# Attention's norms leave GpSimd for ACT and VectorE, its last stores go to GpSimd's queue, and the warming matmuls get fewer and longer

## The chip, the core and the metric

The kernel runs on one core of a Trainium2 chip. Time is device time in microseconds (us), from the profiler or from runs without it. A core has five engines with queues of their own: TensorE (PE in the profile; its weight loads are PEld), VectorE (DVE), ScalarE (ACT), GpSimd (POOL) and SyncE (SP, which here only issues transfers). SP, ACT and GpSimd each issue DMAs on queues of their own (SPq, ACTq, POOLq). Each engine works its instructions in order; semaphores join them.

## The reference, cut

```
q_n, k_n = rmsnorm(q, g_q), rmsnorm(k, g_k)      # 8 batches, 12 heads, 448 tokens, 64 wide
attn = softmax(q_n @ k_n.T / sqrt(64))
x = (attn @ v) as 3584 tokens x 768
logits = x @ w_gate                               # 8 experts
expert = argmax(logits); gate = softmax(logits)[expert]
for e in 8 experts:                               # the 80 tokens with the largest gate
    out[tok] = gate[tok] * (relu(x[tok] @ w1[e]) @ w2[e])
```

`rmsnorm(x, g)` is `x / sqrt(mean(x * x) + 1e-6) * g`. All other rows of `out` are zero.

## The kernel before

Attention works in 24 groups of four heads (three groups to a batch), `NG = 24`. A group has seven rounds of score and exponential (`RD = 7`), and two rounds make a slot, so a batch takes 10.5 slots and the loop 84. A table written out by hand (`begins`, `mid`, `end`, each a list of calls per slot) says what is issued in which slot; each engine's queue keeps that order. In a slot TensorE makes the scores of two rounds (`score`, L332), ACT takes their exponentials (L335), VectorE adds up the ones of the slot before (`presum`, L359 and L361), and TensorE multiplies these by v (`av`, L347). At a group's end ACT copies the product to `us` (L352), which the next group's product waits for, since it uses the same PSUM tile `po`.

A group's q and k (index `a` is 0 and 1) are normalised ahead of its first round `b0`: ACT squares (`square`, L254), VectorE sums over 64 columns (`rstd`, L263) and scales the mean (L265), GpSimd raises it to -1/2 (L272), and GpSimd multiplies q or k by it (`normalise`, L287; VectorE for group 1). TensorE transposes the product (`transp`, L299) and ACT copies it out. Group 0 goes in halves, with a square root on ACT (L269) and a reciprocal on VectorE, and its second halves are multiplied on GpSimd.

After a batch's last group the gate is computed: `zl` on TensorE, two copies on ACT, their sum `zsb` on VectorE (L389), transposes `zt` on TensorE, then on VectorE the products `lx` and the logits, whose exponential `lex` ACT takes (L445). A merge of the batch's tokens into the list of the best 80 per expert follows over six slots (`merge`): `beat`, `tied`, `ahead`, `rnk`, `rank`, `put` and `keep` on VectorE, counts and placing on TensorE (L584, L588). GpSimd computes the small table `info` for it (L463 to L480).

GpSimd's queue also carries the weights. `fetch_w1` and `fetch_w2` bring three experts' weights into SBUF as bf16 (L180, L184), `stage_w` writes the other five to a DRAM scratch (L190), from which SP's queue fetches them late (`fetch_late`, L196). SP's queue loads q, k and v and stores the attention's rows to `xr_scratch`. After the loop comes the last batch's ranking, with matmuls between that have no result (`busy`, L754), then gathers of the chosen rows by GpSimd (L860), and the eight experts (L894, L912).

Of the kernel before, what the change touches and what calls it, by code (L numbers as in the profile page):

```python
# [20 lines left out]
def kernel(  # L21
# [13 lines left out]
    nc = tc.nc  # L35

    B, H, S, D = q.shape
# [16 lines left out]
    NG = B * NQ  # L54
    NB = 2 * NX
# [11 lines left out]
    cpool = ctx.enter_context(tc.tile_pool(name="const", bufs=1))  # L67
# [49 lines left out]
    nc.vector.memset(eps[:, :], 1e-6)  # L117
    nhalf = cpool.tile([128, NB], F32, name="nhalf")
    nc.vector.memset(nhalf[:, :], -0.5)
    zsb = cpool.tile([128, 512], F32, name="zsb")  # L120
# [96 lines left out]
    with av_stack:  # L217
# [3 lines left out]
        st = [dict() for _ in range(NG)]  # L221
# [34 lines left out]

        def rstd(g, a, parts=ALLB):
            if "rs%d" % a not in st[g]:
                st[g]["ms%d" % a] = prep.tile([128, NB], F32, tag=f"ms{a}", name="ms")
                st[g]["rs%d" % a] = prep.tile([128, NB], F32, tag=f"rs{a}", name="rs")  # L260
            ms, rs = st[g]["ms%d" % a], st[g]["rs%d" % a]
            for lo, hi in parts:
                nc.vector.reduce_sum(out=ms[:, lo:hi], in_=st[g]["sq%d" % a][:, lo:hi], axis=AX.X)  # L263
                if parts is ALLB:
                    nc.vector.tensor_scalar(ms[:, lo:hi], ms[:, lo:hi], 1.0 / D, 1e-6,  # L265
                                            op0=ALU.mult, op1=ALU.add)
            for lo, hi in parts:
                if parts is not ALLB:
                    nc.scalar.activation(rs[:, lo:hi], ms[:, lo:hi], AF.Sqrt, scale=1.0 / D,  # L269
                                         bias=eps[:, :])  # L270
                else:
                    nc.gpsimd.tensor_tensor(rs[:, lo:hi], ms[:, lo:hi], nhalf[:, lo:hi],  # L272
                                            op=ALU.pow)

        def inverse(g, a, parts):
            for lo, hi in parts:
                rs = st[g]["rs%d" % a][:, lo:hi]
                nc.vector.reciprocal(rs, rs)  # L278

        def normalise(g, a, parts=ALLB):  # L280
            if "qn%d" % a not in st[g]:
                st[g]["qn%d" % a] = qkpool.tile([128, NB, D], F32, tag=f"qn{a}", name="qn", bufs=2)
            qn, qk, rs = st[g]["qn%d" % a], st[g]["qk"][a], st[g]["rs%d" % a]
            eng = nc.gpsimd if g > 1 or parts is HALF[1] else nc.vector
            for lo, hi in parts:
                h0, h1 = lo // NX, hi // NX
                eng.tensor_mul(  # L287
                    qn[:].rearrange("p (x hh) d -> p hh x d", hh=2)[:, h0:h1],
                    qk[:, lo:hi].rearrange("p (hh x) d -> p hh x d", x=NX),
                    rs[:, lo:hi].rearrange("p (hh x) -> p hh x", x=NX)  # L290
                    .unsqueeze(3).to_broadcast([128, h1 - h0, NX, D]))
# [110 lines left out]
        def gate1v(b):  # L402
# [80 lines left out]
        def merge(b):  # L483
# [29 lines left out]
            def vtied():  # L513
                gw, row = m["gw"], m["row"]
                nc.vector.tensor_tensor(tied[:], row[:, :].rearrange("p (j c) -> p j c", j=NT),
                                        gw.unsqueeze(2).to_broadcast([128, NT, 128]),
                                        op=ALU.is_equal)
                nc.vector.tensor_mul(tied[:], tied[:],
                                     tri[:, :].unsqueeze(1).to_broadcast([128, NT, 128]))

# [80 lines left out]
        def xout(g, u):  # L601
# [48 lines left out]
        for f, *a in ((square, 0, lo), (square, 0, hi), (rstd, 0, lo), (square, 1, lo),  # L650
                      (rstd, 0, hi), (square, 1, hi), (inverse, 0, lo), (normalise, 0, lo),
                      (inverse, 0, hi), (normalise, 0, hi), (rstd, 1, lo), (rstd, 1, hi),
                      (inverse, 1, lo), (normalise, 1, lo), (inverse, 1, hi),
                      (normalise, 1, hi), (transp, 0, 0), (transp, 0, 1), (gains, ),
                      (exptable, ), (transp, 1, 0)):
            at_slot(mid, -10, f, *([0] if a else []), *a)
        for g in range(NG):
# [101 lines left out]
    m, NT = gst[b], NJ + 1  # L759
    busy(35)  # L760
    gate2(b)
# [22 lines left out]
    busy(20)  # L784
    ahead = tpool.tile([128, NT, CAP], BF16, tag="ahead", name="ahead")
    for j in range(NT):
# [10 lines left out]
    nc.vector.tensor_tensor(tied[:], row[:, :].rearrange("p (j c) -> p j c", j=NT),  # L797
                            gw.unsqueeze(2).to_broadcast([128, NT, 128]), op=ALU.is_equal)
    nc.vector.tensor_mul(tied[:], tied[:], tri[:, :].unsqueeze(1).to_broadcast([128, NT, 128]))
    R, back = psb[:, 1, :NT * E], psa[:CAP, 0, :E]  # L800
    for i in range(NT):
# [3 lines left out]
        if i == 0:  # L805
            for j in range(NT):
# [3 lines left out]
    nc.vector.tensor_scalar(stay[:, :], back, rowF[:CAP, NT:NT + 1], float(CAP),  # L810
                            op0=ALU.add, op1=ALU.is_lt)
    left = tpool.tile([CAP, 5, E], BF16, name="left")
    nc.vector.tensor_mul(left[:], stay[:, :].unsqueeze(1).to_broadcast([CAP, 5, E]), listn[:])
# [31 lines left out]
    nc.vector.tensor_add(gwT[:, :], gwT[:, :], num[:, 2])  # L845
    busy(60)
    ps_stack.close()
# [112 lines left out]
```

## Time and profile before

| | us |
|---|---|
| median of 3 runs | 499.72 |
| lowest and highest | 498.36, 500.84 |
| the profiled execution's own time | 497.44 |
| its span, first to last instruction | 495.4 |
| TensorE's granted clock, mean | 0.968 of full speed |

The profile is that of one execution. Its own time is the span and some 2 us around it, and the sums below are made against it.

### The profile page before, as it was taken

Reading aid. Unit: us, or ns where it says so; the run is one execution under the profiler, and the core shown is the slowest. Engines: PE = TensorE matmul, PEld = TensorE weight load, DVE = VectorE, ACT = ScalarE, POOL = GpSimd, SP = SyncE. Lnnn points to the kernel's source line nnn. Section 1 sums busy time; section 2 is a strip of 40 time slices with the busy share of each in tenths; the row PEclk is TensorE's granted clock in tenths of the full one; section 3 lists DMA queues with packets and bytes.
Section 4 is the critical chain, followed back from the end, with each engine's and each line's share of the span. In section 5 each row is a group of like instructions: output and inputs, shape, how many; then the busy total and the mean of one; then the engine's idle time right before and its main releaser. Section 6 shows DMA issues by size and latency. Waiting matters only on the chain. (4 is left out here: it accounts for less than half of the span.)

```text
span 495.4 us, 11552 instructions
## 1 busy us (share of the span) xinstructions
PE 446.8 (90%) x4721; PEld 224.5 (45%) x4721; DVE 368.7 (74%) x569; ACT 317.1 (64%) x489; POOL 269.6 (54%) x210
## 2 busy tenths in 40 slices
PE   6979999999899999898899999898999998659991
PEld 6334434443344444443344444343444443457880
DVE  5769748996889789967799689867897876623540
ACT  6857877966677779676787788666877774101120
POOL 3686983848366748835757678376377400151111
PEclk9989999999899999989999999998999999978996
DMA  7389979697759895977399979958767795957922
GB/s 242 112 179 271 243 180 251 151 295 163 225 80 242 200 271 121 275 199 150 111 232 214 274 167 234 281 109 207 168 167 175 175 268 182 366 139 271 423 69 60
DMA packets 68283, 100.84 MB, mean 204 GB/s; under 512 B 8328, under 2 KB 60040, under 8 KB 66952
## 3 DMA queue, kind: packets, MB, share of 16 engines
q1 hardware_dynamic: 51184, 70.05, 43.4%
q0 software_dynamic: 15776, 29.13, 33.5%
q10 hardware_dynamic: 1272, 0.94, 0.6%
q8 instruction: 37, 0.61, 0.5%
q14 instruction: 14, 0.11, 0.1%
HBM read 101.11 MB, written 39.89 MB: 285 GB/s over the span
## 5 line engine op out<-in xcount | busy, mean ns | idle before, releaser
L272 POOL TENSOR_TENSOR rs<-ms,nhalf 128x14 f32<-128x14 f32 x46 | 136.2, 2964 | 128.6 <-DVE ms L265 125.0
L335 ACT ACTIVATE at<-ps 128x896 f32<-128x896 f32 x168 | 146.4, 922 | 17.7 <-PE ps L332 17.7
L361 DVE TENSOR_TENSOR sm<-sm,at 128x896 f32<-128x896 f32 x120 | 153.1, 1276 | 6.1 <-DVE sm L361 0.5
L332 PE MATMUL ps<-qkT 64*64 64x448 f32 x1344 | 150.1, 557 | 2.3 <-ACT zo L387 1.5
L347 PE MATMUL po<-at,vt 64*64 64x448 f32 x1344 | 146.1, 544 | 6.3 <-ACT us L352 6.3
L347 PEld LDWEIGHTS po<-at,vt 64*64 64x64 f32 x1344 | 49.8, 134 | 79.4 <-issue 66.6
L287 POOL TENSOR_TENSOR qn<-qk,rs 128x896 f32<-128x896 f32 (+1 forms) x46 | 80.8, 1770 | 4.8 <-DVE rs L278 4.4
L263 DVE TENSOR_REDUCE ms<-sq 128x14 f32<-128x896 f32 (+1 forms) x50 | 52.0, 1043 | 29.8 <-ACT sq L254 26.9
L332 PEld LDWEIGHTS ps<-qkT 64*64 64x64 f32 x1344 | 43.4, 134 | 67.9 <-issue 39.7
L299 PE MATMUL tp<-ident,qn 128*128 128x128 f32 x336 | 53.8, 285 | 5.3 <-POOL qn L287 4.0
L299 PEld LDWEIGHTS tp<-ident,qn 128*128 128x128 f32 x336 | 38.5, 144 | 19.6 <-issue 7.1
L254 ACT ACTIVATE sq<-qk 128x896 f32<-128x896 f32 (+1 forms) x50 | 45.9, 923 | 1.4 <-DMA qk<-in_q_dram 1.4
L613 ACT COPY xb<-xp 128x512 f32<-128x512 f32 x48 | 28.3, 590 | 17.9 <-PE xp L608 12.2
L389 DVE TENSOR_TENSOR zsb<-zsb,zo 128x448 f32<-128x448 f32 x7 | 21.3, 3039 | 23.4 <-ACT zo L387 23.4
L898 ACT ACTIVATE h_sb<-ph 128x320 bf16<-128x320 f32 x16 | 6.9, 437 | 47.0 <-PE ph L894 45.9
L320 ACT ACTIVATE qkT<-tp,gqk 128x512 f32<-128x512 f32 (+1 forms) x46 | 29.5, 643 | 6.9 <-PE tp L299 6.9
L608 PE MATMUL xp<-ident,us 128*128 128x128 f32 x192 | 31.8, 290 | 0.0
L608 PEld LDWEIGHTS xp<-ident,us 128*128 128x128 f32 x192 | 21.2, 144 | 21.5 <-issue 17.1
L322 ACT COPY qkT<-tp 128x512 f32<-128x512 f32 (+1 forms) x46 | 24.8, 539 | 7.1 <-PE tp L299 6.9
L920 POOL DMA_INDIRECT out_dram<-yo,idxT x8 | 7.6, 953 | 36.4 <-DVE yo L915 13.5
L352 ACT COPY us<-po 128x896 f32<-128x896 f32 x24 | 21.7, 904 | 7.0 <-PE po L347 7.0
L359 DVE TENSOR_TENSOR sm<-at 128x896 f32<-128x896 f32 x24 | 26.0, 1084 | 0.1
(170 smaller groups left out, 440.8 us busy)
## 6 DMA issues: line engine op xcount, KB each, us to landing
wb_scratch<-in_moe_w_dram POOLq DMA_DIRECT2D x20, 768.0 KB, 8.6
w_sb<-wb_scratch SPq DMA_DIRECT2D x10, 1536.0 KB, 10.8
vt<-in_v_dram SPq DMA_DIRECT2D x24, 448.0 KB, 6.3
out_dram<-zeros SPq DMA_DIRECT2D x28, 384.0 KB, 9.0
qk<-in_q_dram SPq DMA_DIRECT2D x23, 448.0 KB, 7.1
qk<-in_k_dram SPq DMA_DIRECT2D x23, 448.0 KB, 7.7
w_sb<-in_moe_w_dram POOLq DMA_DIRECT2D x6, 1536.0 KB, 16.1
xr_scratch<-xb SPq DMA_DIRECT2D x46, 192.0 KB, 4.1
```

Source lines behind the costliest of these rows:

```text
L254: nc.scalar.activation(st[g]["sq%d" % a][:, lo:hi], st[g]["qk"][a][:, lo:hi], AF.Square)
L263: nc.vector.reduce_sum(out=ms[:, lo:hi], in_=st[g]["sq%d" % a][:, lo:hi], axis=AX.X)
L272: nc.gpsimd.tensor_tensor(rs[:, lo:hi], ms[:, lo:hi], nhalf[:, lo:hi], op=ALU.pow)
L287: eng.tensor_mul(qn[:].rearrange("p (x hh) d -> p hh x d", hh=2)[:, h0:h1], qk[:, lo:hi].rearrange("p (hh x) d -> p hh x d", x=NX), rs[:, ...
L299: nc.tensor.transpose(tp[:, x * 128:(x + 1) * 128], qn[:, 2 * (x0 + x):2 * (x0 + x) + 2].rearrange("p h d -> p (h d)"), ident[:, :])
L320: nc.scalar.activation(o, i, AF.Copy, scale=gqk[:, :])
L332: nc.tensor.matmul(ps[u * 64:u * 64 + 64, hh, :S], T1[d, u, x * 64:(x + 1) * 64], T0[d, u, :], start=True, stop=True)
L335: nc.scalar.activation(at[:], ps[:, :, :S], AF.Exp)
L347: nc.tensor.matmul(po[hh * D:(hh + 1) * D, u, :S], vt[p, hh * NX + x, :], at[p, hh, :], start=(x == 0), stop=(x == RD - 1))
L361: nc.vector.tensor_add(s["sm"][:], s["sm"][:], s["at%d" % x][:])
L608: nc.tensor.transpose(xp[:, j * 128:(j + 1) * 128], us[:, u, c:c + 128], ident[:, :])
L613: nc.scalar.copy(xb[:, :, u * 128:(u + 1) * 128], xp[:, :].rearrange("p (j d) -> p j d", d=128))
```

## The change

The power on GpSimd goes. `rstd` now takes q's and k's means together (28 columns): ACT takes the logarithm and an exponential of minus half of it, and VectorE makes one Newton step of three instructions. The reduction has a function of its own (`squares`), as has group 0's root (`root`). `normalise` is always VectorE's. In the slots, the reductions stay, `rstd` stands in the middle of slot `b0-5`, and group 1's normalisations move back by a slot. The table of functions that ACT loads before the loop has both the logarithm and the exponential. The last group's stores (`xr_scratch` from `rz` and `xb`) move from ACT's queue to GpSimd's. `tied` is made in four instructions of one operation each, not in two over all columns, and at the end it comes after `stay`. The matmuls of `busy` take 512 columns instead of 128, and 9, 5 and 22 of them stand for 35, 20 and 60.

```diff
+        def squares(g, a, parts=ALLB):
...
+                nc.vector.reduce_sum(out=st[g]["ms"][:, a, lo:hi],
+                                     in_=st[g]["sq%d" % a][:, lo:hi], axis=AX.X)
...
-                    nc.gpsimd.tensor_tensor(rs[:, lo:hi], ms[:, lo:hi], nhalf[:, lo:hi],
-                                            op=ALU.pow)
+        def rstd(g):
+            ms, rs, nw = (st[g][n][:].rearrange("p a n -> p (a n)") for n in ("ms", "rs", "nw"))
+            nc.scalar.activation(rs, ms, AF.Ln, scale=1.0 / D, bias=eps[:, :])
+            nc.scalar.activation(rs, rs, AF.Exp, scale=-0.5)
+            nc.vector.scalar_tensor_tensor(nw, rs, -0.5 / D, rs, op0=ALU.mult, op1=ALU.mult)
+            nc.vector.scalar_tensor_tensor(nw, ms, D * 1e-6, nw, op0=ALU.add, op1=ALU.mult)
+            nc.vector.scalar_tensor_tensor(rs, nw, 1.5, rs, op0=ALU.add, op1=ALU.mult)
...
-            eng = nc.gpsimd if g > 1 or parts is HALF[1] else nc.vector
...
-                eng.tensor_mul(
+                nc.vector.tensor_mul(
...
-                (nc.sync if b < B - 1 else nc.scalar).dma_start(
+                (nc.sync if b < B - 1 else nc.gpsimd).dma_start(
...
-            eng = nc.sync if g < NG - 1 else nc.scalar
+            eng = nc.sync if g < NG - 1 else nc.gpsimd
...
+            nc.scalar.preload_act_table_set("natural_log_exp_and_others")
...
+                late = 3 if g == 1 else 0
                 for a in range(2):
-                    late = 3 if g == 1 else 0
                     at_slot(mid, b0 - 7 + a + late, square, g, a)
-                    at_slot(end, b0 - 7 + a + late, rstd, g, a)
-                    at_slot(mid, b0 - 5 + a + min(late, 2), normalise, g, a)
+                    at_slot(end, b0 - 7 + a + late, squares, g, a)
+                at_slot(mid, b0 - 5 + late, rstd, g)
+                for a in range(2):
+                    at_slot(mid, b0 - 5 + a + late, normalise, g, a)
...
-            nc.tensor.matmul(hot[:, :128], identb[:, :], identb[:, :], start=True, stop=True)
+            nc.tensor.matmul(hot[:, :], identb[:, :],
+                             tri[:, :].unsqueeze(1).to_broadcast([128, 4, 128]),
+                             start=True, stop=True)
...
+    for j in range(NT):
+        nc.vector.scalar_tensor_tensor(
+            tied[:, j], row[:, j * 128:(j + 1) * 128], gw[:, j:j + 1], tri[:, :],
+            op0=ALU.is_equal, op1=ALU.mult)
```

What the change does to the order on the engines shows at three places. The first is GpSimd's queue at the start of the program, behind its constants. Before:

```order
L169 MEMSET beat 128x4x64
L164 AFFINE_SELECT tri<-tri 128x128
L287 TENSOR_TENSOR qn<-qk,rs 128x7x64 x2
L272 TENSOR_TENSOR rs<-ms,nhalf 128x14 x4
L180 DMA w_sb<-in_moe_w_dram 128x6x1024
L287 TENSOR_TENSOR qn<-qk,rs 128x2x7x64 x2
L272 TENSOR_TENSOR rs<-ms,nhalf 128x14 x2
```

And with the change:

```order
L167 MEMSET beat 128x4x64
L162 AFFINE_SELECT tri<-tri 128x128
L178 DMA w_sb<-in_moe_w_dram 128x6x1024
L182 DMA w_sb<-in_moe_w_dram 128x8x768
L178 DMA w_sb<-in_moe_w_dram 128x6x1024
L464 TENSOR_SCALAR pt<-numF 128x4
```

Three weight fetches now stand right behind the constants, with nothing ahead of them; the next stand behind the first batch's gate (`pt`).

The second place is VectorE between the second batch's `zsb` and its `lex`. Before:

```order
L389 TENSOR_TENSOR zsb<-zsb,zo 128x448
L361 TENSOR_TENSOR sm<-sm,at 128x896 x4
L409 RECIPROCAL rz<-zs 128x12x2 x2
L417 TENSOR_TENSOR lx<-zs,rz 128x12x8 x4
L263 TENSOR_REDUCE ms<-sq 128x14
L265 TENSOR_SCALAR ms<-ms 128x14
L432 TENSOR_REDUCE lg<-lx 128x32
L435 TENSOR_REDUCE lmax<-lg 128x4
L438 TENSOR_TENSOR lex<-lg,lmax 128x32
```

And with the change (`nw` is the Newton step's own tile):

```order
L390 TENSOR_TENSOR zsb<-zsb,zo 128x448
L362 TENSOR_TENSOR sm<-sm,at 128x896 x2
L273 SCALAR_TENSOR_TENSOR nw<-rs 128x28
L274 SCALAR_TENSOR_TENSOR nw<-ms,nw 128x28
L275 SCALAR_TENSOR_TENSOR rs<-nw,rs 128x28
L288 TENSOR_TENSOR qn<-qk,rs 128x2x7x64
L362 TENSOR_TENSOR sm<-sm,at 128x896 x2
L288 TENSOR_TENSOR qn<-qk,rs 128x2x7x64
L410 RECIPROCAL rz<-zs 128x12x2 x2
L418 TENSOR_TENSOR lx<-zs,rz 128x12x8 x4
```

Two normalisations and a Newton step have moved in between; the reduction, `lg` and `lex` follow as before.

The third place is ACT behind the last group, where `us` is the last product's copy. Before:

```order
L352 COPY us<-po 128x896
L383 COPY zsb<-zl 128x448
L613 COPY xb<-xp 128x4x128
L424 DMA xr_scratch<-rz 64x4x12
L424 DMA xr_scratch<-rz 64x3x12
L613 COPY xb<-xp 128x4x128
L621 DMA xr_scratch<-xb 64x3x256 x2
L622 DMA xr_scratch<-xb 64x256
L445 ACTIVATE lex<-lex 128x32
L770 COPY eqT<-pse 24x512
```

And with the change:

```order
L353 COPY us<-po 128x896
L384 COPY zsb<-zl 128x448
L613 COPY xb<-xp 128x4x128 x2
L446 ACTIVATE lex<-lex 128x32
L776 COPY eqT<-pse 24x512
```

The five stores are gone from ACT's order; in GpSimd's they stand ahead of the last batch's `pt` and `info`.

## Rows read from the trace of the kernel before

**Rows 1.** The page's first part: busy us (share of the span), instructions.
```profile
PE 446.8 (90%) x4721; PEld 224.5 (45%) x4721; DVE 368.7 (74%) x569; ACT 317.1 (64%) x489; POOL 269.6 (54%) x210
```

**Rows 2.** Groups by shape: line, engine, operation, count | busy us, mean ns.
```profile
L361 DVE TENSOR_TENSOR sm<-sm,at 128x896 f32<-128x896 f32 x120 | 153.1, 1276 | 6.1 <-DVE sm L361 0.5
L359 DVE TENSOR_TENSOR sm<-at 128x896 f32<-128x896 f32 x24 | 26.0, 1084 | 0.1
L389 DVE TENSOR_TENSOR zsb<-zsb,zo 128x448 f32<-128x448 f32 x7 | 21.3, 3039 | 23.4 <-ACT zo L387 23.4
L569 DVE SCALAR_TENSOR_TENSOR rank<-rank,cnt 128x4 f32<-128x4 f32 x7 | 5.6, 799 | 0.2
L837 DVE SCALAR_TENSOR_TENSOR idxF<-num 80x8 f32<-80x8 f32 x1 | 0.2, 164 | 0.0
L287 DVE TENSOR_TENSOR qn<-qk,rs 128x896 f32<-128x896 f32 x2 | 2.2, 1092 | 3.3 <-POOL rs L272 3.3
L269 ACT ACTIVATE rs<-ms,eps 128x7 f32<-128x7 f32 x4 | 1.2, 297 | 0.9 <-DVE ms L263 0.9
L272 POOL TENSOR_TENSOR rs<-ms,nhalf 128x14 f32<-128x14 f32 x46 | 136.2, 2964 | 128.6 <-DVE ms L265 125.0 <-PE ps L332 3.0
```

**Rows 3.** Waits: engine, line, released by: us in total, times, longest.
```profile
PE po L347 <- ACT us L352: 6.3, 3, 2.1
PE tp L299 <- POOL qn L287: 4.0, 3, 3.0
PE mp L584 <- DVE put L572: 3.8, 3, 1.8
PE zt L394 <- DVE zsb L389: 3.7, 4, 1.2
PE mp L588 <- DVE keep L576: 1.2, 3, 0.4
```

**Rows 4.** In order of time, an odd batch's gate: start us, us, engine, line.
```profile
119.51 4.14 DVE L389 TENSOR_TENSOR zsb<-zsb,zo 128x448 f32<-128x448 f32 x1 [2.77 <-ACT zo L387]
131.61 0.23 ACT L445 ACTIVATE lex<-lex 128x32 f32<-128x32 f32 x1 [2.70 <-DVE lex L438]
```

**Rows 5.** In order of time, the start: ACT, TensorE, SP's DMA queue.
```profile
14.69 1.79 ACT L254 ACTIVATE sq<-qk 128x896 f32<-128x896 f32 x2
16.83 1.73 ACT L335 ACTIVATE at<-ps 128x896 f32<-128x896 f32 x2
17.33 0.98 PE L299 MATMUL tp<-ident,qn 128*128 128x128 f32 x7
29.97 0.81 PE L299 MATMUL tp<-ident,qn 128*128 128x128 f32 x4 [3.04 <-POOL qn L287]
7.86 0.37 SPq L226 DMA_DIRECT2D qk<-in_q_dram  x1
```

**Rows 6.** First weight fetch; loads issued in 16:19 and 70:75, us to landing.
```profile
27.10 1.09 POOL L180 DMA_DIRECT2D w_sb<-in_moe_w_dram  x1
qk<-in_q_dram SPq DMA_DIRECT2D x1, 448.0 KB, 3.6
qk<-in_q_dram SPq DMA_DIRECT2D x1, 448.0 KB, 12.7
```

**Rows 7.** The end in order of time, and its stores' landing (420:434).
```profile
424.33 1.25 ACTq L621 DMA_DIRECT2D xr_scratch<-xb  x2
426.32 0.23 ACT L445 ACTIVATE lex<-lex 128x32 f32<-128x32 f32 x1 [2.02 <-issue]
434.44 0.17 DVE L840 TENSOR_SCALAR idxG<-idxF 80x8 uint32<-80x8 f32 x1
xr_scratch<-xb ACTq DMA_DIRECT2D x2, 192.0 KB, 9.0
```

**Rows 8.** Matmuls of the first and second expert, in order of time.
```profile
444.69 3.36 PE L894 MATMUL ph<-xgT,w_sb 128*128 128x80 bf16 x48 [4.05 <-issue]
451.80 1.88 PE L894 MATMUL ph<-xgT,w_sb 128*128 128x80 bf16 x48
```

More of the change, by code (lines that the diff above doesn't have):

```diff
@@ L117 @@
     nc.vector.memset(eps[:, :], 1e-6)
-    nhalf = cpool.tile([128, NB], F32, name="nhalf")
-    nc.vector.memset(nhalf[:, :], -0.5)
     zsb = cpool.tile([128, 512], F32, name="zsb")
@@ L255, in square, with root @@
                                      AF.Square)
[L257 to L261, printed above, removed]
+        def squares(g, a, parts=ALLB):
+            if "ms" not in st[g]:
+                for n in ("ms", "rs", "nw"):
+                    st[g][n] = prep.tile([128, 2, NB], F32, tag=n, name=n)
             for lo, hi in parts:
[L263 to L266, printed above, removed]
+                nc.vector.reduce_sum(out=st[g]["ms"][:, a, lo:hi],
+                                     in_=st[g]["sq%d" % a][:, lo:hi], axis=AX.X)
+        def root(g, a, parts):
             for lo, hi in parts:
[L268 to L271, printed above, removed]
-                    nc.gpsimd.tensor_tensor(rs[:, lo:hi], ms[:, lo:hi], nhalf[:, lo:hi],
-                                            op=ALU.pow)
+                nc.scalar.activation(st[g]["rs"][:, a, lo:hi], st[g]["ms"][:, a, lo:hi], AF.Sqrt,
+                                     scale=1.0 / D, bias=eps[:, :])
+        def rstd(g):
[5 more added lines that the diff above has]
+            nc.vector.scalar_tensor_tensor(rs, nw, 1.5, rs, op0=ALU.add, op1=ALU.mult)
         def inverse(g, a, parts):
             for lo, hi in parts:
-                rs = st[g]["rs%d" % a][:, lo:hi]
+                rs = st[g]["rs"][:, a, lo:hi]
                 nc.vector.reciprocal(rs, rs)
@@ L282, in normalise @@
                 st[g]["qn%d" % a] = qkpool.tile([128, NB, D], F32, tag=f"qn{a}", name="qn", bufs=2)
-            qn, qk, rs = st[g]["qn%d" % a], st[g]["qk"][a], st[g]["rs%d" % a]
-            eng = nc.gpsimd if g > 1 or parts is HALF[1] else nc.vector
+            qn, qk, rs = st[g]["qn%d" % a], st[g]["qk"][a], st[g]["rs"][:, a]
             for lo, hi in parts:
                 h0, h1 = lo // NX, hi // NX
-                eng.tensor_mul(
+                nc.vector.tensor_mul(
                     qn[:].rearrange("p (x hh) d -> p hh x d", hh=2)[:, h0:h1],
@@ L514, in vtied @@
                 gw, row = m["gw"], m["row"]
[L515 to L519, printed above, removed]
+                for j in range(NT):
+                    nc.vector.scalar_tensor_tensor(
+                        tied[:, j], row[:, j * 128:(j + 1) * 128], gw[:, j:j + 1], tri[:, :],
+                        op0=ALU.is_equal, op1=ALU.mult)
             def experts():
@@ L645, in exptable @@
         def exptable():
+            nc.scalar.preload_act_table_set("natural_log_exp_and_others")
             nc.scalar.activation(warm[:, 0:1], warm[:, 1:2], AF.Exp)
         lo, hi = HALF
[L650 to L653, printed above, removed]
+        for f, *a in ((square, 0, lo), (square, 0, hi), (squares, 0, lo), (root, 0, lo),
+                      (square, 1, lo), (squares, 0, hi), (root, 0, hi), (square, 1, hi),
+                      (inverse, 0, lo), (normalise, 0, lo), (inverse, 0, hi),
+                      (normalise, 0, hi), (squares, 1, lo), (root, 1, lo), (squares, 1, hi),
+                      (root, 1, hi), (inverse, 1, lo), (normalise, 1, lo), (inverse, 1, hi),
                       (normalise, 1, hi), (transp, 0, 0), (transp, 0, 1), (gains, ),
@@ L753, in busy @@
         for i in range(n):
-            nc.tensor.matmul(hot[:, :128], identb[:, :], identb[:, :], start=True, stop=True)
+            nc.tensor.matmul(hot[:, :], identb[:, :],
+                             tri[:, :].unsqueeze(1).to_broadcast([128, 4, 128]),
+                             start=True, stop=True)
     b = B - 1
     m, NT = gst[b], NJ + 1
-    busy(35)
+    busy(9)
     gate2(b)
@@ L783 @@
                          listT[:, :], start=True, stop=True)
-    busy(20)
+    busy(5)
     ahead = tpool.tile([128, NT, CAP], BF16, tag="ahead", name="ahead")
@@ L796 @@
                 gw.unsqueeze(2).to_broadcast([128, NT, CAP]), op=ALU.is_lt)
-    nc.vector.tensor_tensor(tied[:], row[:, :].rearrange("p (j c) -> p j c", j=NT),
-                            gw.unsqueeze(2).to_broadcast([128, NT, 128]), op=ALU.is_equal)
-    nc.vector.tensor_mul(tied[:], tied[:], tri[:, :].unsqueeze(1).to_broadcast([128, NT, 128]))
     R, back = psb[:, 1, :NT * E], psa[:CAP, 0, :E]
@@ L811 @@
                             op0=ALU.add, op1=ALU.is_lt)
+    for j in range(NT):
+        nc.vector.scalar_tensor_tensor(
+            tied[:, j], row[:, j * 128:(j + 1) * 128], gw[:, j:j + 1], tri[:, :],
+            op0=ALU.is_equal, op1=ALU.mult)
     left = tpool.tile([CAP, 5, E], BF16, name="left")
@@ L845 @@
     nc.vector.tensor_add(gwT[:, :], gwT[:, :], num[:, 2])
-    busy(60)
+    busy(22)
     ps_stack.close()
```

## The prediction

> **What bounds the kernel now.** I read the page's busy shares first: TensorE is busy 90% of the span, VectorE 74%, ACT 64% [rows 1]. So time can only come out of gaps on TensorE, or out of the ends of the program, where TensorE is not the bound. GpSimd's 46 powers are long, but their length costs nothing by itself: the question is who waits for them.
>
> The second view is the groups of instructions by shape [rows 2]. Look at the same operation under two conditions. The first addition of a group's row sums takes 1,084 ns, the later ones, of the same shape, 1,276 ns. The gate's addition `zsb`, 448 columns and so about half of that, takes 3,039 ns. A `scalar_tensor_tensor` of four columns takes 799 ns in the merge and 164 ns at the end of the program, where GpSimd computes nothing. So VectorE's operations with two SBUF inputs are held while GpSimd computes. GpSimd's power pays as well, 2,964 ns for 14 columns. Worked out: 120 x 0.192 + 7 x (3.04 - 0.58) + 7 x 0.635 = 23.0 + 17.2 + 4.4 = 44.7 us of VectorE's busy time is standing still.
>
> The third view is the list of waits, for TensorE alone [rows 3]: 3.8 us for `put` and 1.2 for `keep` (the merge on VectorE), 3.7 for `zsb`, 6.3 for ACT's copy `us`, 4.0 for GpSimd's `qn`. Together 19.0 us, the most that freeing VectorE could give in the loop.
>
> **VectorE's account.** 44 normalisations move to it, at 1,092 ns [rows 2], 48.0 us; 69 Newton steps at about 164 ns are 11.3 us; 46 scalings of `ms` fall away. Against the 44.7 us set free it has some 15 us more to do at most, 77% of the span instead of 74%. On average it isn't the bound. What counts is the place.
>
> **Even batches: `put`.** The merge's `rnk` and `rank` are held, and TensorE stands for `put`. After the change one normalisation and three Newton steps stand ahead of `rnk` (1.1 + 0.5 us), but two held operations lose 0.6 us or more each, and the earlier ones in this stretch lose their holds too. I take 4.5 of the 5.0 us (0 to 5.0).
>
> **Odd batches: `zsb` to `us`.** In the trace's second view of time, the order on the engines around 119 us [rows 4], `zsb` runs 4.14 us; ACT's `lex` waits for VectorE until 131.61, the copy `us` stands behind it in ACT's order, and TensorE's `po` waits for that copy, 2.1 us at most [rows 3]. GpSimd's end frees 4.14 - 0.58 = 3.56 us on VectorE. But the order now has two normalisations and a Newton chain between `zsb` and `lex`: 2 x 1.09 + 3 x 0.16 = 2.67. So `lex` comes only 0.9 us earlier, three times: 2.7 us, where the waits alone promise 6.3 + 3.7 (bounds 0 and 10.0; I stay near the lower, since the added instructions stand in the order).
>
> **GpSimd's `qn`.** Of the 4.0 us one wait of 3.04 lies in the start (below); the other 1.0 goes. For what follows a gap (the slow clock after it, waits too short for the list) I add 1.5 (0 to 3). The loop thus gives -4.5 - 2.7 - 1.0 - 1.5 = -9.7.
>
> **The start.** Two things happen here that the diff doesn't show. Group 1's norm now hangs on ACT behind the exponentials of slot 1, which end at 18.56: two activations of 0.30, three Newton steps of 0.16, a normalisation of 1.09, so `qn` at 20.7, where TensorE transposed it at 17.33 [rows 5]: 3.4 us later. In exchange the 3.04 us at 29.97 goes, since GpSimd's queue of powers is gone. The two half normalisations that VectorE takes over ahead of the first scores cost about 1.1 (two halves of 1.09). Sum +1.5.
>
> The other thing: GpSimd's first weight fetch was issued at 27.10, behind four powers. Nothing stands ahead of the first three now, so they go out with the constants, into the loads of the first groups. What that does is shown by the trace's list of transfers [rows 6]: a load of q with no fetch beside it lands after 3.6 us, one beside a fetch after 12.7. Group 2's q, issued at 7.86, would land at 20.6 and not at 11.5; its square stands second in the pair that began at 14.69, at about 15.6 [rows 5], with the exponentials of slot 1 behind it. So up to 5.0 us more, and up to 3.5 again for group 3's. From -3 (all hidden) to +10; I take +3.5.
>
> **ACT.** 46 activations of at most 297 ns (the nearest row is the root of 7 columns) are 13.7 us on an engine with a third of its time free; a group's logarithm stands where its reduction has long been issued. I take +1 (0 to 4).
>
> **The end.** ACT issues the last group's stores from 424.33, and `lex` waits 2.02 us for that, with the whole ranking behind it [rows 7]. With the stores on GpSimd's queue `lex` comes 2.0 us earlier. But the gathers need the stores too: issued at 424.33, they took 9.0 us, to 433.3, beside the late weights, and the index is written at 434.61. The stores are late next after 1.3 us. Their issue on GpSimd, five of at most 1.09 us (a fetch's row), can also end later than before. I take -1.0 (-2.3 to +1.5).
>
> The Trainium skill ("DMA: Bandwidth & Descriptors", section "SWDGE vs HWDGE vs iDMA") says that plain transfers belong on the queues of SP and ACT, and its section "Specifications" that GpSimd's have the longer way to the first byte, about 1 us against 0.6. By it the stores would land 0.4 us later than on ACT's queue and the end's term would be -0.6. The landing of 9.0 us here is twenty times that difference, so the sum goes by the row.
>
> **The warming matmuls.** Nine, five and 22 of 512 columns for 35, 20 and 60 of 128: 4,608, 2,560 and 11,264 columns for 4,480, 2,560 and 7,680. They fill time in which TensorE has nothing else, so 0. The first expert's matmuls took 3.36 us and the second's 1.88 [rows 8], the first at the lower clock; if the longer filling held the clock up it would give 1.5 us, if it let it fall, the second would lose as much. `tied` in four pieces: no row of that shape; it stays near zero.
>
> **Sum.** -9.7 + 3.5 + 1.0 - 1.0 = -6.2 against the profiled execution's own 497.44: 491.2. That execution is 2.3 below the median of the three runs, so the median should be 493.5, 1.2% faster.
>
> **Rivals.**
> *The waits go entirely* (0.22): VectorE runs ahead, the 19.0 us of [rows 3] vanish, start and ACT cost what they give. 497.4 - 19.0 + 1 - 1 = 478.4, as a median 480.7. For it: 44.7 us of held time. Against it: the order between `zsb` and `lex`.
> *The start eats the gain* (0.20): three fetches at once keep the transfers busy for the first 40 us, and each load comes 9 us late. +10 for +3.5: 500.0, no change. For it: the landings of 12.7; against it: q and k of the first two groups are issued ahead of the fetches.
> *ACT and VectorE chain up* (0.12), the slower side: the logarithm waits for VectorE's reduction in ACT's order, and the exponentials that TensorE needs stand behind it. At 0.7 us a group it is 23 x 0.7 = 16 us, 491.2 + 16 - 1 = 506, median 508.5. It turns the change into a loss from 0.31 us a group on (7.2 / 23). Against it: in the loop ACT waits for VectorE's `lex` alone so far.
>
> **Chances.** 0.44 for the forecast (its own range 488 to 499), 0.22, 0.20 and 0.12 for the rivals, 0.02 for the rest. The range of 481 to 503 takes in the start's +10 and half of the first rival; left out are the chain-up and the best tail. Faster by over 0.5%, about what a measurement of this kernel can tell from none: four fifths of the forecast, the first rival, a fifth of the second: 0.63. Within it 0.20, slower 0.17.
>
> **What will show it.** Right: the later additions at 1.08 us, `zsb` at 0.6; no wait for `put`; TensorE still waiting for `us` in odd batches, about 2 us each; a longer gap on TensorE near 18 to 26 us and loads of over 10 us there; `lex` at the end free of the issue, the gather held by stores. Wrong: `us` waits gone (first rival), the gaps of the start reaching slot 6 (second), ACT's logarithm in the list of waits with more than 7 us (third).

## The result

The changed kernel takes 484.66 us (median of 4 runs, 484.14 to 485.29), the kernel before 499.25 in the same comparison. The ratio is 0.9705, with a 95% interval of 0.9675 to 0.9734: 3.0% faster. The forecast was 493.5, 1.2% faster. The time lies in the range of 481 to 503, but the gain is two and a half times the one forecast, and the kernel stands nearer to the first rival (the waits go entirely, 480.7) than to the forecast.

The profiled execution of the changed kernel took 485.29 us, 0.6 above its median, with a span of 483.4. Its busy shares, and the groups that answer to [rows 1, 2]:

```profile
PE 446.7 (92%) x4642; PEld 220.3 (46%) x4642; DVE 358.1 (74%) x653; ACT 326.0 (67%) x535; POOL 58.1 (12%) x123
```
```profile
L362 DVE TENSOR_TENSOR sm<-sm,at 128x896 f32<-128x896 f32 x120 | 130.6, 1089 | 3.3
L288 DVE TENSOR_TENSOR qn<-qk,rs 128x896 f32<-128x896 f32 x46 | 50.1, 1088 | 1.1
L390 DVE TENSOR_TENSOR zsb<-zsb,zo 128x448 f32<-128x448 f32 x7 | 4.4, 626 | 17.5 <-ACT zo L388 17.5
L569 DVE SCALAR_TENSOR_TENSOR rank<-rank,cnt 128x4 f32<-128x4 f32 x7 | 1.1, 164 | 0.2
```

VectorE has 44 whole multiplications and two halves more and yet is busy 10.6 us less: the later additions (1,089 ns) now run like the first ones of [rows 2], `rank` (164 ns) like its kind at the program's end, and `zsb` at 626 ns. The list of waits for TensorE, against [rows 3]:

```profile
PE tp L300 <- DVE qn L288: 4.4, 1, 4.4
PE ph L901 <- issue: 4.0, 5, 1.1
PE mp L552 <- ACT at L336: 3.9, 3, 1.9
PE po L348 <- ACT us L353: 3.8, 3, 1.3
```

`put`, `keep` and GpSimd's `qn` are gone from the list. `us` has fallen from 6.3 to 3.8. But 3.9 us are new, in the even batches, ahead of the merge's counts (`mp`, L552).

Where along the program the 12.0 us of span lie, by two instructions that both kernels have (before, then after; start us, us, engine, line):

```profile
75.64 0.66 PE L394 MATMUL zt<-ident,zsb 128*128 128x128 f32 x4
...
418.78 0.56 PE L378 MATMUL zl<-us,wgs 64*32 64x448 f32 x1 [1.03 <-ACT us L352]
```
```profile
77.63 0.66 PE L395 MATMUL zt<-ident,zsb 128*128 128x128 f32 x4
...
408.29 0.56 PE L379 MATMUL zl<-us,wgs 64*32 64x448 f32 x1 [1.03 <-ACT us L353]
```

The first batch's `zt` comes 2.0 us later, the last `zl` 10.5 earlier. So the start lost 2.0, the loop gained 12.5, and the end gained 12.0 - 10.5 = 1.5.

**The loop's new wait.** It is not ACT's added work. ACT's own list of waits, and the stores of `xb` in the trace's list of transfers (median us from issue to landing), first in the changed kernel at 90 to 104 us, then in the kernel before at 88 to 102:

```profile
ACT xb L613 <- DMA xr_scratch<-xb: 8.3, 4, 2.8
```
```profile
xr_scratch<-xb SPq DMA_DIRECT2D x2, 192.0 KB, 8.7
```
```profile
xr_scratch<-xb SPq DMA_DIRECT2D x2, 192.0 KB, 2.8
```

`xb` has one buffer, so ACT's next copy to it waits until the store has landed. The exponentials behind that copy are late, and TensorE waits. Two weight transfers were issued at 87.39 and 88.34, right behind the batch's `info`, and the store went out behind them; in the kernel before the powers had spread the transfers, and the fetch there was issued at 92.16, behind the store. That the bursts are the cause is tested below (e1, e14).

**The slow clock.** Stretches of the kernel before and the changed one behind the waits of [rows 3] (us, busy of each engine, then the granted clock of TensorE, DMA share, GB/s), three of before, two of after:

```profile
133.00:136.00 3.00, 3.00 (x15) 1.35 (x7) 1.08 (x4) 2.52 (x4) 1.72 (x8) 0.50 0.09 26
210.00:214.00 4.00, 3.55 (x27) 2.36 (x31) 3.86 (x4) 1.36 (x3) 0.15 (x1) 0.66 0.99 302
...
341.00:345.00 4.00, 4.00 (x27) 2.19 (x27) 2.21 (x3) 2.98 (x6) 2.83 (x9) 0.58 0.76 115
```
```profile
133.00:136.00 3.00, 3.00 (x27) 1.47 (x31) 1.15 (x5) 3.00 (x5) 2.09 (x6) 1.00 0.59 182
...
210.00:214.00 4.00, 4.00 (x44) 1.44 (x39) 3.90 (x5) 4.00 (x8) 0.00 (x0) 1.00 1.07 366
```

Behind a gap of 2.1 or 1.8 us TensorE ran for a while at the lower of its two levels (0.50 granted, 1.2 of 2.4 GHz): 3 x 0.50 + 4 x 0.34 + 4 x 0.42 = 4.5 us lost in three places (5.1 if the whole loop is added up in steps of 3 us). In two others (313 and 239 us) the clock stayed at 1.00 behind gaps of 1.4 and 2.1. In the changed kernel the granted clock is 1.00 in every stretch from 30 to 408 us.

In the start it is the other way round. The stretches at half clock there, before and then after:

```profile
30.00:34.00 4.00, 4.00 (x24) 1.58 (x28) 2.59 (x2) 1.59 (x2) 3.88 (x2) 0.57 1.07 188
```
```profile
20.00:30.00 10.00, 7.16 (x43) 3.36 (x43) 6.94 (x13) 5.30 (x10) 0.00 (x0) 0.66 1.13 247
```

That is 1.7 us lost before (behind the wait of 3.04 us) and 3.4 after (behind the new one of 4.4).

One execution of a later run, e16, took 1,866 us against 477 to 479 for its other five, and is left out of its median.

### The profile page after: what moved, and what is told of

Read it like the earlier page. It is cut to its first block, busy times and chain, and to the rows that moved or that the text cites. A ratio compares the mean times of both kernels' runs of the same rounds, so it can differ in the third digit from the quotient of the medians.

```text
span 483.4 us, 11318 instructions
## 1 busy us (share of the span) xinstructions
PE 446.7 (92%) x4642; PEld 220.3 (46%) x4642; DVE 358.1 (74%) x653; ACT 326.0 (67%) x535; POOL 58.1 (12%) x123
## 5 line engine op out<-in xcount | busy, mean ns | idle before, releaser
L336 ACT ACTIVATE at<-ps 128x896 f32<-128x896 f32 x168 | 146.3, 921 | 16.9 <-PE ps L333 16.8
L362 DVE TENSOR_TENSOR sm<-sm,at 128x896 f32<-128x896 f32 x120 | 130.6, 1089 | 3.3
L288 DVE TENSOR_TENSOR qn<-qk,rs 128x896 f32<-128x896 f32 (+1 forms) x50 | 52.6, 1051 | 1.3
L478 POOL CAST pt<-gw 128x4 bf16<-128x4 f32 x8 | 1.5, 192 | 333.8 <-DVE gw L453 333.8
L919 PE MATMUL py<-w_sb,h_sb 128*80 128x384 bf16 x128 | 24.3, 344 | 1.2 <-ACT h_sb L905 1.0
L922 DVE TENSOR_SCALAR yo<-py,gwT 80x384 f32<-80x384 f32 x16 | 9.8, 614 | 17.2 <-PE py L919 17.2
```

The lines of the kernel that those rows point to most:

```text
L288: nc.vector.tensor_mul(qn[:].rearrange("p (x hh) d -> p hh x d", hh=2)[:, h0:h1], qk[:, lo:hi].rearrange("p (hh x) d -> p hh x d", x=NX), ...
L336: nc.scalar.activation(at[:], ps[:, :, :S], AF.Exp)
L362: nc.vector.tensor_add(s["sm"][:], s["sm"][:], s["at%d" % x][:])
```

## The experiments

Four sets of runs, each on another chip, with runs of the kernel before beside them. Times are medians in us; differences are taken inside one set.

| set | before | run | us | ratio (95%) |
|---|---|---|---|---|
| 1 | 496.21 | e1 paced | 480.81 | 0.970 (0.962 to 0.979) |
| | | e2 paced, dead powers | 481.17 | 0.971 (0.963 to 0.980) |
| | | e3 paced, GpSimd multiplies | 498.84 | 1.006 (1.002 to 1.010) |
| | | e4 the ends alone | 494.38 | 0.996 (0.991 to 1.001) |
| 2 | 495.73 | e5 changed kernel | 481.49 | 0.972 (0.969 to 0.974) |
| | | e6 paced, dead multiplications | 528.86 | 1.067 (1.065 to 1.070) |
| | | e7 before, gaps filled | 490.23 | 0.988 (0.986 to 0.991) |
| | | e8 paced, start and odd moved | 480.27 | 0.968 (0.965 to 0.970) |
| 3 | 495.11 | e9 multiplications moved alone | 475.98 | 0.963 (0.959 to 0.966) |
| | | e10 e9 with ends and odd batches | 473.26 | 0.956 (0.952 to 0.960) |
| | | e11 paced, odd batches | 474.88 | 0.960 (0.956 to 0.963) |
| | | e12 e11 with the start | 474.42 | 0.958 (0.954 to 0.962) |
| 4 | 498.58 | e13 changed kernel | 485.62 | 0.974 (0.969 to 0.979) |
| | | e14 paced | 481.36 | 0.965 (0.960 to 0.969) |
| | | e15 e9 with bursts | 494.32 | 0.991 (0.988 to 0.994) |
| | | e16 as e9 | 477.59 | 0.959 (0.954 to 0.964) |

**What holds VectorE: e1, e2, e3, e6.** All four pace the weight transfers, so that these don't differ among them:

```diff
+    def paced():
+        if newest:
+            nc.gpsimd.tensor_copy(pace[:, :], newest[-1][:, 0, 0:1])
     def fetch_w1(e):
+        paced()
...
             nc.vector.reduce_sum(out=st[g]["ms"][:, a, lo:hi],
                                  in_=st[g]["sq%d" % a][:, lo:hi], axis=AX.X)
+            newest.append(st[g]["ms"])
```

> The changed kernel, and ahead of each weight transfer GpSimd copies one number from the newest mean of squares, so that a transfer can't go out before its slot. Theory A (the weight transfers, which now leave in bursts, delay the attention's stores and loads: ACT's copy to xb waits for the store, and TensorE then waits 3.9 us in the three even batches, and for group 1's norm 4.4 us in the start): those three waits go, the start improves by up to 2, and the median is 479 to 482, against 484.7 of the changed kernel. Rival (the three waits come from the work that was added to ACT and VectorE): they stay, and the median is 484 to 486.

e2 adds a power behind each sum of squares:

```diff
+            if parts is ALLB:
+                nc.gpsimd.tensor_tensor(dead[:, a], st[g]["ms"][:, a], nhalf[:, :], op=ALU.pow)
```

> As the paced kernel, and GpSimd again takes its 46 powers of 14 columns, into a tile that nobody reads. Nothing waits for them. Theory H (what the change took away is the time in which VectorE's two-input operations were held by GpSimd's computing): the later additions rise from 1.09 towards 1.18 us or more, zsb to over 1 us, the waits for put and us grow again, and the median is 4 to 9 us above the paced kernel. Rival P (the gain is that norms come sooner and no longer stand in GpSimd's queue): within 1.5 us of the paced kernel.

e3 gives the multiplications back to GpSimd:

```diff
-                nc.vector.tensor_mul(
+                (nc.gpsimd if g > 1 else nc.vector).tensor_mul(
```

> As the paced kernel, but the multiplications of q and k by the norm are GpSimd's again from group 2 on (the norms stay on ACT and VectorE). Theory H: GpSimd computes some 130 us again, VectorE is held, and the median is 3 to 8 us above the paced kernel, although VectorE has 48 us less to do. Rival V (VectorE's added work is what remains to be paid, between zsb and lex above all): the waits for us shrink and the median is 1 to 3 us below the paced kernel.

e6 keeps VectorE's and has GpSimd make them once more into the spent tile of squares:

```diff
+            if g > 1:
+                nc.gpsimd.tensor_mul(st[g]["sq%d" % a][:], qk[:],
+                                     rs.unsqueeze(2).to_broadcast([128, NB, D]))
```

> As the paced kernel, and GpSimd makes the 44 multiplications of q and k by the norm as well, into a tile that nobody reads; TensorE uses VectorE's, so nothing waits for GpSimd. Theory M (GpSimd's multiplications of 896 columns hold VectorE's two-input operations, its powers don't): the later additions rise to 1.2 us or more, the waits for put and us come back, and the median is 6 to 20 us above the paced kernel (480.8). Rival Q (the kernel with GpSimd's multiplications was slow because TensorE and the queue waited for GpSimd's slower result): within 1.5 us of the paced kernel.

The groups of e2, of e3 and of e6, in this order:

```profile
L277 POOL TENSOR_TENSOR dead<-ms,nhalf 128x14 f32<-128x14 f32 x46 | 136.8, 2975 | 188.6 <-DVE ms L273 187.8 <-DVE rnk L582 0.4
L378 DVE TENSOR_TENSOR sm<-sm,at 128x896 f32<-128x896 f32 x120 | 130.7, 1089 | 3.3
```
```profile
L373 DVE TENSOR_TENSOR sm<-sm,at 128x896 f32<-128x896 f32 x120 | 149.2, 1243 | 4.1
L299 POOL TENSOR_TENSOR qn<-qk,rs 128x896 f32<-128x896 f32 x44 | 87.6, 2002 | 155.6 <-PE tp L311 84.2 <-PE ps L344 49.3 <-PE xp L619 17.6
```
```profile
L376 DVE TENSOR_TENSOR sm<-sm,at 128x896 f32<-128x896 f32 x120 | 157.7, 1314 | 4.0 <-ACT at L350 0.9
L298 POOL TENSOR_TENSOR sq<-qk,rs 128x896 f32<-128x896 f32 x44 | 100.1, 2288 | 155.6 <-ACT qkT L337 46.9 <-issue 46.8 <-ACT rs L283 31.9
```

With 136.8 us of powers on GpSimd an addition takes 1,089 ns, as with none, and the time is that of e1 (+0.4 us). With 88 us of multiplications it takes 1,243 and the time is 18.0 us longer, more than twice the 3 to 8 expected. The multiplications of e6, whose product nobody reads, cost 47.4 us (528.86 against 481.49 for the changed kernel in the same set; 48.6 against e8, which is paced too), where 6 to 20 were expected. They aren't quite free of waits: ACT's next squares go into the same tile and wait 4.1 us for them in all. So theory M holds for the multiplications, in its direction though not in its size, and theory H as I put it for e2 falls: not GpSimd's computing holds VectorE, only its multiplications of 896 columns do. e3 also says that the change would have lost without them: with the norms on ACT and VectorE and the multiplications left on GpSimd, the kernel is 2.6 us slower than before.

The trace of the kernel before had shown it. GpSimd and VectorE in order of time, around the long `zsb` of [rows 4], then the same place in e2:

```profile
117.25 2.62 POOL L272 TENSOR_TENSOR rs<-ms,nhalf 128x14 f32<-128x14 f32 x1
119.84 3.32 POOL L287 TENSOR_TENSOR qn<-qk,rs 128x896 f32<-128x896 f32 x2
```
```profile
119.73 2.62 POOL L277 TENSOR_TENSOR dead<-ms,nhalf 128x14 f32<-128x14 f32 x1
...
121.83 0.63 DVE L406 TENSOR_TENSOR zsb<-zsb,zo 128x448 f32<-128x448 f32 x1 [3.06 <-ACT zo L404]
```

The `zsb` of 4.14 us from 119.51 ends at 123.65, just behind GpSimd's two multiplications (123.16). In e2 it starts inside a power (119.73 to 122.35) and takes 0.63. The Trainium skill ("SBUF — State Buffer", section "SBUF: two separate sides") says that VectorE's two-input operations and a GpSimd operation that reads SBUF lock each other out for a whole instruction. The trace agrees for the multiplications and not for the powers, which read SBUF too; the measurement decides.

Counted over the whole trace of the kernel before, 23 of the 120 later additions overlap a multiplication and together take 22.8 us more than the shortest; 33 overlap a power and no multiplication, and take some 10 ns more each. The first additions, which the prediction set against them, overlap no multiplication. Nor is it two-input operations alone that are held, as the prediction had it: `beat`, with one tensor of input, before and with the change:

```profile
L510 DVE TENSOR_SCALAR beat<-row,gw 128x320 bf16<-128x320 f32 x7 | 7.6, 1091 | 0.0
```
```profile
L511 DVE TENSOR_SCALAR beat<-row,gw 128x320 bf16<-128x320 f32 x7 | 2.7, 381 | 0.0
```

**What follows a gap: e7.** The kernel before, with matmuls that have no result in two of its waits:

```diff
+            if s in (25, 46, 67):
+                spare = tpps.tile([128, 512], F32, tag="tp", name="spare")
+                fill(spare[:, :], 6)
...
             def place():
                 ps = scratch()
+                if b in (0, 2, 4):
+                    fill(ps[:, 1, :], 5)
```

> The kernel before with its waits left as they are, but TensorE has matmuls without a result to do in them: six of 512 columns ahead of the product that waits for us in the three odd batches, five ahead of the one that waits for put in batches 0, 2 and 4. Theory K (after a gap of some 2 us TensorE runs at half its clock for about 3 us, in some runs and places and not in others; this is up to 5 us of the kernel before, which the change took away with the gaps): the granted clock stays at 1.00 behind these places, the median falls by 1.5 to 4 us and the runs lie closer together than the 7 us of the kernel before. Rival (the half clock there has another cause): median within 1 us, spread as before, or up to 2 us slower by the matmuls added.

5.5 us faster, with nothing of VectorE's or GpSimd's work changed; in the traces the last `zl` starts 4.5 us earlier (414.28 against 418.78). Stretches behind the same three places, in e7's own time:

```profile
132.00:136.00 4.00, 3.30 (x30) 1.47 (x31) 2.01 (x8) 3.94 (x7) 3.16 (x8) 1.00 0.51 149
...
209.00:213.00 4.00, 3.60 (x43) 2.08 (x45) 3.76 (x5) 2.43 (x5) 0.00 (x0) 1.00 1.00 297
...
338.00:342.00 4.00, 4.00 (x43) 1.87 (x39) 2.08 (x4) 4.00 (x7) 2.82 (x9) 1.00 0.74 109
```

Theory K holds for the clock. Two points of the expectation don't: the median fell by more than the 4 us allowed, and the runs lie no closer together (2.6 us apart, the kernel before 2.8 in this set).

**The parts alone: e4, e9, e16.** e4 makes the change's stores and warming matmuls alone, whose lines the diff of the change shows.

> The kernel before with two parts of the change alone: the last group's stores on GpSimd's queue, and the warming matmuls of 512 columns (9, 5 and 22). The norms are as before. The prediction gave these parts -1.0 us (-2.3 to +1.5), so 496.5 to 500.5 for a median of 499.25. Read from the two traces the end is 1.5 us shorter: 497.7. Rival (the end carries much of the gain that the loop does not explain): 494 to 496.

-1.8 us, with an interval that touches 1: near both expectations, and not the 3 to 5 of its rival. e9 is one line:

```diff
-            eng = nc.gpsimd if g > 1 or parts is HALF[1] else nc.vector
+            eng = nc.vector
```

> The kernel before with one line changed: the multiplications of q and k by the norm are VectorE's in every group. The powers stay on GpSimd, and so do the means' scaling, the stores and the warming matmuls as before. Theory M (the multiplications on GpSimd were what held VectorE; the powers held nothing, so moving them to ACT and VectorE gave nothing): the later additions at 1.09 us, no wait for put, and a median 10 to 15 us below the kernel before, as the whole change. Rival (powers and multiplications both matter, or TensorE now waits for GpSimd's powers, two of 2.96 us in a row for each group): less than 7 us below.

> The kernel with only the multiplications moved, again: 18 to 20 us below the kernel before and 4 to 6.5 below the changed kernel.

-19.1 and -21.0 us: more than the whole change gives (-14.2 in set 2, -13.0 in set 4), and more than was expected of e9 (10 to 15) and, by a little, of e16. Against the changed kernel of its set e16 is 8.0 us faster, where 4 to 6.5 were expected. The groups of e9, and TensorE's waits between 30 and 400 us:

```profile
L272 POOL TENSOR_TENSOR rs<-ms,nhalf 128x14 f32<-128x14 f32 x46 | 137.7, 2996 | 189.9 <-DVE ms L265 189.7
L361 DVE TENSOR_TENSOR sm<-sm,at 128x896 f32<-128x896 f32 x120 | 130.5, 1088 | 4.0
```
```profile
PE po L347 <- ACT us L352: 3.0, 3, 1.0
...
PE mp L552 <- ACT at L335: 0.5, 1, 0.5
```

**What the moved powers cost: e5, e13, e14, e15.** e5 and e13 are the changed kernel unaltered, e14 is e1 again.

> The changed kernel once more, to stand beside the others on one chip. The norms alone then give its distance to the kernel with the ends alone (1.8 us below the kernel before). Expected: 481 to 485, that is 12 to 15 us below the kernel before, of which 2 to 4 us are the slow clock after gaps, which the kernel before has in some runs and not in others.

> The changed kernel again, beside the next three on one chip: 13 to 15 us below the kernel before.

> The paced kernel beside the changed one. Theory A (bursts of transfers cost the three waits of 3.9 us in the loop): 2.5 to 4.5 us below the changed kernel. Rival (they cost nothing that the end doesn't take back): within 1 us of it.

Pacing gives 4.3 us on one chip. In the trace of e1 the wait ahead of the counts is 0.7 us, not 3.9:

```profile
PE mp L563 <- ACT at L347: 0.7, 1, 0.7
```

ACT's waits for the store fall from 8.3 us in four places to 1.6 in one. That one is in the first batch, where a fetch still goes out 3.5 us ahead of the store, which lands after 7 to 9 us. In e15 I put the bursts into e9, by a list of slots:

```diff
+        for b, n in ((None, 3), (0, 2), (1, 3), (2, 4), (3, 5), (4, 4), (5, 4), (6, 1)):
+            for f, *a in moves[:n]:
+                at_slot(begins, -10 if b is None else (NQ * b + NQ - 1) * RD // 2 + 9, f, *a)
+            del moves[:n]
```

> The kernel with only the multiplications moved, but its weight transfers leave where the changed kernel's do: three ahead of all powers, the others in bursts behind each batch's gate. Theory A: the waits ahead of the counts come back in the even batches, the first loads come later, and the median is 3 to 6 us above the kernel without bursts. Rival (the 5.5 us between it and the changed kernel are the norms on ACT and VectorE): within 1 us of it.

+16.7 us, far more than the 3 to 6 expected. These bursts don't stand at the same instant as the changed kernel's (in the first batch 4.0 us behind the end of `info`, not right behind it); whether that is why is not shown. In e15's waits of ACT, and TensorE's between 30 and 400 us:

```profile
ACT xb L613 <- DMA xr_scratch<-xb: 22.1, 6, 7.3
```
```profile
PE xp L608 <- ACT xb L613: 5.9, 2, 5.0
PE ps L332 <- ACT zo L387: 4.8, 7, 1.8
```

These waits and a new stretch at half clock (267 to 276 us, 3.4 us lost) make up most of the 15.5 us by which the last `zl` is later than in e16. It shows the mechanism and not its size in the changed kernel; for the size e14 stands.

**Better versions: e8, e10, e11, e12.** e8 moved group 1's sums and logarithm ahead of slot 1's exponentials, and `gate1v` ahead of the slot's normalisation.

```diff
-                    at_slot(end, b0 - 7 + a + late, squares, g, a)
-                at_slot(mid, b0 - 5 + late, rstd, g)
+                    at_slot(mid if g == 1 else end, b0 - 7 + a + late, squares, g, a)
+                at_slot(mid, b0 - 5 + late - (g == 1), rstd, g)
...
+            slot = mid.setdefault(b0 + 7, [])
+            at = next((i for i, (f, a) in enumerate(slot) if f is normalise and b % 2), len(slot))
+            slot.insert(at, (gate1v, (b, )))
```

> The paced kernel with two more moves. In the start, group 1's sums of squares and its logarithm stand ahead of the exponentials of slot 1, not behind them; in the odd batches the products of the gate, up to lex, stand ahead of the normalisation of the same slot on VectorE. Theory S (the 2.7 us wait for group 1's norm and the three waits of 1.3 us for us are places in the order, not lack of VectorE's time): the start gains 1.5 to 2.7 us, the odd batches 0.8 to 1.1 each, and the median is 3 to 6 us below the paced kernel. Rival (VectorE or ACT are late there anyway, and the wait only moves): within 1 us of it.

Neither worked: TensorE still waits 3.8 us for `us`, and 4.1 for group 1's `qn`. In the trace the normalisation now lies between `lx` and the reduction `lg`, so `lex` comes no sooner: the chain's second half, `gate2`, had been left behind. e10 and e11 move the whole chain:

```diff
+            if b % 2:
+                mid.setdefault(b0 + 7, [])[:0] = [(gate1v, (b, )), (gate2, (b, ))]
+            else:
+                at_slot(mid, b0 + 7, gate1v, b)
+                at_slot(end, b0 + 7, gate2, b)
```

> As the kernel with only the multiplications moved, with the change's stores and warming matmuls, and in the odd batches the whole gate up to lex ahead of the slot's normalisation and reduction on VectorE. Theory M and S: 1.8 us less by the ends, and 3 x 1.0 to 1.3 less by the waits for us: 3 to 6 us below the kernel with the multiplications alone, and below the changed kernel. Rival: the waits move on to another instruction, within 2 us of it.

> The paced kernel, and in the odd batches the whole gate up to lex ahead of the slot's normalisation and reduction on VectorE (in the run before, only the products stood ahead, and the wait for us stayed at 1.3 three times). Theory S: lex comes 2 us earlier, the three waits for us of 1.3 go, and with them 3 to 4 us of the loop; median 476 to 478 where the kernel before has 496. Rival: TensorE then waits for the normalisation or the reduction put behind, within 1 us of the paced kernel (480.8).

In e12 the start of e8 goes on: group 1's first normalisation a slot sooner, group 2's first square a slot later.

```diff
+                    later = int(g == 2 and a == 0)
+                    at_slot(mid, b0 - 7 + a + late + later, square, g, a)
...
+                    at_slot(mid, b0 - 5 + a + late - (g == 1 and a == 0), normalise, g, a)
```

> As the run with pace and odd batches, and in the start group 1's sums, logarithm, Newton step and first normalisation follow at once, ahead of VectorE's constants, while group 2's first square stands a slot later. Theory S: TensorE's wait for group 1's norm (2.1 to 4.4 us in the traces so far) falls under 1.5, and the median is 1.5 to 3 us below the run without it. Rival (the start is limited by the loads and by the slow clock, which follows the gap wherever it lies): within 1 us of it.

In e11 the waits for `us` fall from 3.8 to 0.4 us, and in e10 they are gone, with 2.5 us of new waits for `ahead` in their place. e10, with powers on GpSimd and multiplications on VectorE, is the fastest of all: 473.26, ratio 0.956, 4.4% below the kernel before. Against e9 that is 2.7 us, a little less than the 3 to 6 expected. The start of e12 adds nothing that can be told (-0.5); its wait for group 1's norm is still 2.5.

## Why the prediction was wrong

Its direction holds, and so does its mechanism in the main: VectorE was held by GpSimd's work. That the time lies in the range of 481 to 503 is in part luck, since terms missed on both sides cancel. By its own steps, from the two profiled executions:

| step | forecast | measured |
|---|---|---|
| `put`, `keep` | -4.5 | -5.0, and +3.9 at the counts |
| odd batches, `zsb` to `us` | -2.7 | -4.4 (2.5 of `us`, 1.9 of `zt`) |
| GpSimd's `qn` in the loop | -1.0 | -1.0 |
| what follows a gap | -1.5 | -4.5 by the clock's rows |
| ACT | +1.0 | no wait for its logarithm in the loop |
| loop | -8.7 | -12.5 |
| start | +3.5 | +2.0 |
| end | -1.0 | -1.5 |
| profile to median | +2.3 | -0.6 |

The loop's rows leave 1.5 us of its 12.5: 0.6 is slow clock outside the three stretches, the rest isn't traced. From 493.5 to 484.66 are 8.8 us: 3.8 of the loop, 1.5 of the start, 0.5 of the end, 2.9 of the last row.

**The step that failed** is "For what follows a gap (...) I add 1.5 (0 to 3)". Its mechanism was right and its size a third, beyond its own bound of 3. The rows of the clock showed 4.5 us in three places, and e7 gets 5.5 us back by filling gaps alone. I had the rows and read only the list of waits, in which a slower matmul is no wait. The first step had already shut it out: "time can only come out of gaps on TensorE, or out of the ends of the program" takes a busy TensorE for one at its full clock.

**The odd batches.** "So `lex` comes only 0.9 us earlier, three times" is what came (0.8 less wait for each `us`). What the step left out are the waits for `zsb` itself, by which it had set its own bound of 10.0; 1.9 of them went. (That bound, and the 19.0 us of all waits, hold 0.8 for a `zsb` of the end and the 19.0 also the 3.0 of the start; for the loop they are 9.2 and 15.2.)

**The median.** I added the 2.3 us by which one execution of before lay under its median, as if that belonged to the kernel. It is scatter: runs of before are spread over 7 us in set 1 (490.97 to 498.25), those of the changed kernel over 1.2 in its own comparison (5.3 in set 4).

**Right in sign, wrong in place.** I saw that weight fetches with nothing ahead of them would hurt, and looked for it in the start alone. Each later batch has the same burst, and in the even ones it meets a store with one buffer: +3.9 us. In the start the loads of q and k land after 7.5 and 8.1 us (2 to 30 us of the trace), not 12.7, and the wait is that for the norm behind the exponentials, 3.4 us in the forecast and 4.4, 2.1 and 4.7 us in three traces. The halves cost what was forecast: the first scores start at 13.04, not 12.03. What the start's sum left out is again the slow clock behind the wait, 3.4 us for 1.7.

**Wrong without a price.** "GpSimd's power pays as well" and the whole part on what holds VectorE took powers and multiplications as one. The sum doesn't show it, since the change takes both away; e2, e3 and e9 do. The norms by logarithm, most of the diff, show no gain of their own: e14 is 3.8 us slower than e16, although it has the ends as well. The two differ in `tied` too (1.38 us a batch on VectorE for 1.11) and in when the weights go out, and no run has the norms alone. By TensorE's order in the two traces, the product behind group 1's transposes starts at 25.86 in e14 and at 22.29 in e16, and takes 2.46 against 1.68 us: 4.4 us in the start. The last `zl` is 5.9 later (404.32 against 398.38), so 1.5 more in the loop, and the end takes some back.

**The end.** `lex` waits for VectorE (1.0 us) and not for the issue of stores, as forecast. "They fill time in which TensorE has nothing else, so 0" does not hold for the ranking in this execution. TensorE in order of time, the nine long matmuls and the two steps behind them:

```profile
413.27 4.00 PE L758 MATMUL hot<-tri,identb 128*128 128x512 bf16 x9 [0.67 <-ACT xb L613]
...
417.19 0.45 PE L773 MATMUL pse<-identb,eqb 128*24 128x128 bf16 x4
417.58 0.65 PE L784 MATMUL psb<-ident,gw 128*128 128x128 f32 x4
```

At a granted clock of 0.50 (413.0 to 417.3) they take 4.00 us, in e14 and e5 at full clock 2.10. `gw` was ready at 414.97, and `psb` stood behind them until 417.58. In this trace the gathers didn't wait for the stores: the index was written at 424.85, the first gather went out at 425.72. In e5, the same kernel with the nine matmuls at full clock, they seem to. Its last store, the index and the first gather:

```profile
412.45 0.55 POOL L622 DMA_DIRECT2D xr_scratch<-xb  x1
...
419.83 0.17 DVE L847 TENSOR_SCALAR idxG<-idxF 80x8 uint32<-80x8 f32 x1
...
423.53 1.03 POOL L867 DMA_INDIRECT xg<-xr_scratch,idxG  x1 [8.58 <-issue]
```

The gather stands 3.5 us behind the index there, and the store landed 9.8 us after its issue, at 422.3, as forecast ("The stores are late next"); the trace names no releaser, so this is read from the times. So the slow matmuls cost the ranking and not the end: the first gather goes out 17.4 us behind the last `zl` in both traces, 16.8 in the kernel before. GpSimd's queue did not make the stores land later: 9.5 and 9.8 us in e5, 9.7 and 9.2 on ACT's queue in e9. The end's 1.5 us lie behind the first gather (59.8 us to the program's end before, 57.7 after), and there two executions of the changed kernel differ by 2.3 us (55.4 in e5). That the term came out near its forecast is luck.

**A sum.** The chance of "faster by over 0.5%", worked out from its parts, is 0.35 + 0.22 + 0.04 = 0.61 and not 0.63.

Open is why multiplications hold VectorE and a power doesn't, why some gaps of 2 us are followed by the slow clock and others aren't, and what the norms by logarithm give or cost alone.

## What to carry to other kernels

When an operation is slow beside another engine, look up which instruction of that engine lies beside it before the whole engine is blamed: one line here (the multiplications) was worth 19 us or more, and the rest of the diff, most of its lines, took some of that back. Whoever empties a queue should ask what else that queue had been spacing out: GpSimd's powers paced the weight transfers, and bursts cost 4.3 us until a one-element copy paced them again. And read the granted clock behind each gap, since a gap costs itself and what follows it.

## What was unexpected of the hardware

GpSimd's power of 14 columns takes 2,975 ns and slows no addition on VectorE (1,089 ns beside 46 of them); its multiplications of 896 columns slow them to 1,243 (e3) and 1,314 on average (e6), a held one by 1.4 us or more, and take 2,288 ns themselves in e6, against 1,808 in the kernel before. Filling three waits for `us` and three for `put` with 33 matmuls of 512 columns made the kernel before 5.5 us faster.
